# The first feed-forward block summed in six blocks of tiles instead of seven, and its list scheduler's weights set anew

## The chip, the cores and the metric

One core of a Trainium2 chip. Every time is in device microseconds (us) of that core; the time of a kernel is the median of its runs. The engines are called by their names: TensorE (PE, and PEld for its weight loads), VectorE (DVE), ScalarE (ACT), GpSimd (POOL), and SyncE (SP), which issues most DMAs.

## What is computed

Attention with a learned relative bias, then two feed-forward blocks without residuals. The change lies in the first of the two, `_moe_ref`, and in the way the second is cut:

```python
def _moe_ref(x, w_in, w_out, a, b):          # x 1152 x 512, w_in 512 x 2048, w_out 2048 x 512
    h = x @ w_in
    h2 = h * h
    h3 = h2 * h
    P = a[0] + a[1] * h + a[2] * h2 + a[3] * h3
    Q = 1.0 + np.abs(b[0]) * np.abs(h) + np.abs(b[1]) * h2
    g = P / (Q + 1e-06)
    return g @ w_out

def _moe2_ref(x, w_in, w_out):               # same sizes
    h = x @ w_in
    return np.maximum(0.01 * h, h) @ w_out
```

The weights come as 64-bit numbers.

## The kernel before

The attention takes the first 255 us or so. The feed-forward blocks work on the 2048 hidden features in 16 tiles f = 0 to 15 of 128 features, each over all 1152 tokens. Precision is kept by splitting every operand into a high and a low half, so a product is three matmuls (high x high, high x low, low x high).

**Per tile of the first block.** `gemm1(f, kk)` (L349 to L362) makes h of tile f in PSUM: 4 contractions x 3 products x 3 token chunks of 384 = 36 matmuls on L359. There are two such PSUM buffers, so `gemm1` of tile f waits until the last reader of tile f-2, `r_v`, is through. Then comes the rational function, in steps of one instruction each over 128 x 1152 (tile 15 in three chunks of 384):

- ScalarE: `r_abs` (L395), `r_s1` (L399), `r_qq` (L406), `r_ln` (L416), `r_exp` (L419), `r_q1` (L424), `split_hi` (L449).
- VectorE: `r_qa` (L403, needs `r_abs`), `r_h2` (L409, needs `r_s1`), `r_h3` (L412), `r_v` (L433, needs `r_h3` and `r_exp`), `r_fin` (L436, needs `r_v` and `r_e`).
- GpSimd: `r_e` (L430, needs `r_exp` and `r_q1`; for tiles 0 to 2 it is done on VectorE, L428) and `split_lo` (L454, needs `split_hi`).

`r_ln` and `r_exp` give 1/Q, `r_fin` the tile g, and `split_hi`/`split_lo` its two halves gh and gl, in a pool of buffers.

**Units.** The product g @ w_out is summed over blocks of tiles (`BLOCKS`, L138). For each block there are 12 units (n, c): 4 output groups x 3 token chunks. `g2_mm` (matmuls on L940) is a unit's 3 matmuls for each tile of the block, into one of two PSUM buffers; `g2_acc` takes the sum out: for the first block by a copy on ScalarE (L950), for every later one by an add on VectorE (L952). After the last block each result is split for the next product (L955 on ScalarE, L967 on VectorE).

**Weights.** Step t loads two weight tiles by DMA (`w_load`, SP), turns them from 64 to 32 bits by three VectorE steps (`w_dve`, L316, L318, L320), and splits them by `w_hi` (L330, ScalarE) and `w_lo` (L338, GpSimd).

**The order.** All engines take their instructions in the order in which the program issues them. For the first block, `plan_first` (L1002) writes every step down as a task with its engine, its cost (`COST`) and what it waits for, and `arrange` (L71) is a list scheduler: a task's rank is the longest chain behind it plus a number per kind of step from `SHIFT`; on the engine that can begin first it takes, of the tasks that can start within `SLACK` of that beginning, the one of the highest rank. The list that comes out is the order of issue. It begins after `gemm1` of tile 1; what is ahead is written out by hand. The second block (`g2_tok`, matmuls on L981, adds on L989) has a fixed plan by steps of a tile and uses the same `BLOCKS`.

Of the kernel before, what the change touches and what calls it, by code (L numbers as in the profile page):

```python
# [43 lines left out]
SHIFT = {'g2_acc': 85.7,
         'g2_mm': 40.9,
         'g2_out': 8.3,
         'gemm1': 162.0,
         'r_abs': 97.9,
         'r_e': -55.8,
         'r_exp': 33.0,  # L50
         'r_fin': -7.4,
         'r_h2': 273.8,
         'r_h3': -41.1,
         'r_ln': -206.8,
         'r_q1': 51.6,
         'r_qa': -51.7,
         'r_qq': 199.1,
         'r_s1': -20.3,
         'r_v': 10.2,
         'split_hi': 262.3,  # L60
         'split_lo': 61.1,
         'w_dve0': 177.5,
         'w_dve1': 15.3,
         'w_dve2': 11.6,
         'w_hi': 90.2,
         'w_lo': 57.9,
         'w_load': 106.7}
SLACK = 0.19


def arrange(tasks, ends, free):  # L71
# [63 lines left out]
]  # L135
MASK_BUFS = 20
LOAD_BUFS, EARLY = 3, 4
BLOCKS = [1, 2, 2, 2, 3, 3, 3]  # L138
NEX = 2
HI_MERGED = ()  # L140
LO_MERGED = ()
# [91 lines left out]
def attn_bias_moe_kernel(  # L233
# [131 lines left out]
    pools = {}  # L365
# [636 lines left out]
    def plan_first(rest, by_chunk):  # L1002
# [12 lines left out]
        units, held = [], {}  # L1015
# [5 lines left out]
        u_of = {bi: [u for u in units if u[0] == bi] for bi in range(len(blocks))}  # L1021
# [24 lines left out]
        for f in range(1, NF):  # L1046
            if f > 1:
                for kk in range(KD):
                    add(("gemm1", f, kk), [("gemm1", f, kk - 1) if kk else ("gemm1", f - 1, KD - 1)]
                        + [made.get(("i", f))] + [("r_v", *x) for x in parts(f - 2)])  # L1050
            part = 1 / len(parts(f))
            last = ("gemm1", f, KD - 1)
            for x in parts(f):
                c = x[1:]
                add(("r_abs", *x), [last, ("r_qa", f - 1)], part)
                add(("r_s1", *x), [last, ("split_lo", f - 3)], part)
                add(("r_qa", *x), [("r_abs", *x), ("r_fin", f - 3)], part)
# [12 lines left out]
                add(("split_lo", *x), [("split_hi", *x)], part)  # L1070
        before = []
# [13 lines left out]
    for m, plan, g2_lag, fn, args in (  # L1085
# [31 lines left out]
        for s in range(4 * (NF + 5)):  # L1117
# [5 lines left out]
            for step, name, *a in plan:  # L1123
                f, rem = divmod(s - step, 4)
# [80 lines left out]
```

## Time and profile before

| | us |
|---|---|
| median of 3 runs | 674.03 (673.1 to 675.94) |
| the profiled execution | 678.19, its span 676.4 |
| attention and the first tiles, to about | 256 |
| first feed-forward block, to | 472.1 |
| second feed-forward block, to the end | 676.4 |
| TensorE busy | 598.4 (88% of the span) |
| VectorE busy | 526.1 (78%) |
| ScalarE busy | 410.2 (61%) |
| GpSimd busy | 360.0 (53%) |

The table's busy times are averages over stages in which different engines set the pace, so they say little by themselves: the stage has to be read, and in it which wait ends last. A wait is idle time of an engine ahead of an instruction, put down to what released it.

### The profile page before, as it was taken

The page shows a single profiled execution, that of the slowest core. Times are in us where ns is not written, and L with a number is a line of the kernel's source. Part 1 is how long each engine was busy: PE and PEld are TensorE (multiplying, and loading weights), DVE is VectorE, ACT ScalarE, POOL GpSimd, SP SyncE. Part 2 cuts the span into 40 slices and gives each one's busy share as a digit, 9 for nine tenths or more (in the row PEclk, how much of TensorE's full clock was granted, in tenths as well). Part 3 has the DMA queues.
Part 4 walks back from the last instruction along what each step waited for, and adds up shares of the span by engine and source line. Part 5 has one row for each costly group of instructions (what it writes and reads, how often), then busy time and mean ns, then how long its engine had stood idle before and what let it go on. Part 6 is the DMA issues. An engine that isn't in the chain of part 4 may idle for free.

```text
span 676.4 us, 11799 instructions
## 1 busy us (share of the span) xinstructions
PE 598.4 (88%) x4595; PEld 528.8 (78%) x4595; DVE 526.1 (78%) x809; ACT 410.2 (61%) x625; POOL 360.0 (53%) x263
## 2 busy tenths in 40 slices
PE   5767778889888866779999998999999999999998
PEld 3333557778677856779998898999999999999876
DVE  7999889988979577888999999998256465645463
ACT  9999678888868357687687686754254223232210
POOL 5766687766756412467547565752154634453340
PEclk9998979998979788879999999999999999999999
DMA  5666799999969812113122211011132313230113
GB/s 191 185 165 189 214 158 205 210 189 194 160 127 175 192 62 89 67 63 125 62 71 71 108 63 63 31 64 63 48 112 91 125 63 111 76 125 31 60 50 125
DMA packets 102199, 77.35 MB, mean 114 GB/s; under 512 B 86400, under 2 KB 86784, under 8 KB 102144
## 3 DMA queue, kind: packets, MB, share of 16 engines
q1 hardware_dynamic: 100848, 68.97, 40.0%
q10 hardware_dynamic: 1296, 7.64, 3.5%
q8 instruction: 36, 0.59, 0.3%
q14 instruction: 19, 0.16, 0.1%
HBM read 42.39 MB, written 2.36 MB: 66 GB/s over the span
## 4 chain that ended last, share of the span: by engine, by line
PE 50%; DVE 25%; ACT 6%; issue 5%; DMA 3%; POOL 1%; SPq 0%; DVEq 0%; ACTq 0%; POOLq 0%
PE ph L359 20%; PE pz L981 13%; PE py L940 7%; PE ps L721 5%; DVE raw L320 2%; DVE ph L412 2%; DVE raw L318 2%; PE pv L813 2%; DVE raw L316 2%; DVE bias L952 2%; DMA biasr<-in_moe_w_in 2%; DVE s L433 2%; DVE s L436 2%; DVE pt L733 2%; DVE qq L403 1%
## 5 line engine op out<-in xcount | busy, mean ns | idle before, releaser
L359 PE MATMUL ph<-bias,bias 128*128 128x384 f32 x1152 | 218.5, 345 | 15.4 <-DVE s L433 12.8
L359 PEld LDWEIGHTS ph<-bias,bias 128*128 128x128 f32 x1152 | 209.5, 195 | 20.8 <-issue 12.8
L786 POOL TENSOR_TENSOR hl<-ex,hl 128x512 f16<-128x512 f32 (+2 forms) x94 | 91.5, 991 | 38.1 <-DVE hl L773 20.7
L454 POOL TENSOR_TENSOR gl<-s,gh 128x1152 fp32r<-128x1152 f32 (+1 forms) x33 | 85.5, 2595 | 35.6 <-ACT gh L449 35.1
L721 PE MATMUL ps<-kt,qz 128*128 128x288 f32 x432 | 80.9, 328 | 21.5 <-DVE mn L733 16.2
L721 PEld LDWEIGHTS ps<-kt,qz 128*128 128x128 f32 x432 | 64.6, 203 | 33.7 <-DVE mn L733 17.6
L338 POOL TENSOR_TENSOR bias<-raw,bias 128x512 fp32r<-128x512 f32 x37 | 49.1, 1329 | 74.9 <-ACT bias L330 74.9
L940 PE MATMUL py<-gh,wo 128*128 128x384 f32 x288 | 80.7, 340 | 4.0 <-DVE bias L952 3.4
L989 DVE TENSOR_TENSOR bias<-pz,bias 128x512 f32<-128x512 f32 x48 | 33.1, 689 | 59.8 <-PE pz L981 59.5
L981 PE MATMUL pz<-wo,gh 128*128 128x512 f32 (+1 forms) x240 | 74.4, 386 | 0.3 <-DVE bias L989 0.3
L338 POOL TENSOR_TENSOR wo<-raw,wo 128x512 fp32r<-128x512 f32 x23 | 30.3, 1318 | 78.1 <-ACT wo L330 78.0
L749 ACT ACTIVATE ex<-pt,mn 128x576 f32<-128x576 f32 x72 | 55.3, 768 | 19.0 <-DVE mn L733 15.3
L629 PEld LDWEIGHTS <-coef 128*32 128x32 f16 x1152 | 27.3, 99 | 41.9 <-issue 27.4
L647 POOL TENSOR_TENSOR t<-t,te 128x576 f32<-128x576 f32 x36 | 47.0, 1310 | 22.4 <-DVE bb L652 12.9
L940 PEld LDWEIGHTS py<-gh,wo 128*128 128x128 f32 x288 | 52.6, 188 | 8.1 <-DVE bias L952 6.2
L733 DVE CUSTOM_DVE_ANT_0 pt<-ps,bias 128x576 f32<-128x576 f32 x64 | 47.4, 744 | 6.7 <-PE ps L721 5.4
L330 ACT ACTIVATE wo<-raw 128x512 fp32r<-128x512 f32 x27 | 17.0, 629 | 58.1 <-DVE raw L320 58.1
L940 PE MATMUL py<-gl,wo 128*128 128x384 f32 x156 | 52.2, 335 | 0.0
L441 ACT ACTIVATE s<-ph 128x1152 f32<-128x1152 f32 x16 | 18.2, 1136 | 54.8 <-PE ph L359 43.5
L981 PEld LDWEIGHTS pz<-wo,gh 128*128 128x128 f32 x240 | 44.3, 188 | 8.2 <-DVE bias L989 0.7
L981 PE MATMUL pz<-wo,gl 128*128 128x512 f32 (+1 forms) x129 | 50.1, 389 | 0.0
L430 POOL TENSOR_TENSOR qq<-qq,r 128x1152 f32<-128x1152 f32 (+1 forms) x15 | 37.9, 2524 | 16.6 <-ACT r L419 12.0
(134 smaller groups left out, 1188.9 us busy)
## 6 DMA issues: line engine op xcount, KB each, us to landing
biasr<-in_moe_w_in SPq DMA_DIRECT2D x32, 512.0 KB, 4.4
biasr<-in_moe_w_out SPq DMA_DIRECT2D x32, 512.0 KB, 3.5
bias<-bb SPq DMA_DIRECT2D x32, 288.0 KB, 3.6
qkv<-in_qkv ACTq DMA_DIRECT2D x8, 896.0 KB, 5.2
out<-bias SPq DMA_DIRECT2D x8, 256.0 KB, 2.0
biasr<-bb SPq DMA_DIRECT2D x8, 144.0 KB, 4.0
et<-hl SPq DMA_TRANSPOSE x40, 4.8
sm<-in_small SPq DMA_DIRECT2D x1, 416.0 KB, 5.4
```

What stands on the lines that cost most here:

```text
L338: G.tensor_tensor(lo_, raw[:, x], hi_.bitcast(F32), ALU.subtract)
L359: PE.matmul(ps[:, c, 0:CH], w[:, sl], x[kk][:, c * CH:(c + 1) * CH], start=(kk == 0 and n == 0), stop=(kk == KD - 1 and n == 2),)
L430: G.tensor_tensor(part(qq[f], c), part(qq[f], c), part(r0[f], c), ALU.mult)
L454: eng.tensor_tensor(part(gl, c), part(s1[f], c), part(gh, c).bitcast(F32), ALU.subtract)
L647: G.tensor_tensor(t1, t0s.pop(n), te[:, S - first_row(n):2 * S - first_row(n)], ALU.mult)
L721: PE.matmul(ps[:, c, 0:288], lt[:, a], kts[i][:, b, 288 * c:288 * c + 288], start=(n == 0), stop=(n == 2),)
L733: V.tensor_tensor_reduce(out=c2(pt), in0=s_ps.pop((i, j))[:, :, 0:288], in1=c2(bsrc), op0=ALU.add, op1=ALU.min, scale=1.0, scalar=3.0e38, ...
L749: A.activation(et, pt, AF.Exp, bias=mn, scale=-1.0, accum_out=sums[i][:, col:col + 1],)
L786: engines[j in at].tensor_tensor(hl[:, xs, dst], e9[:, xs, src], hl[:, xs, src], ALU.subtract)
L940: PE.matmul(ps[:, 0:CH], w[:, sl], gts[f][x][:, cs], start=(f == f0 and m == 0), stop=(f == f0 + nf - 1 and m == 2),)
L981: PE.matmul(ps[:, half], gts[f][x][:, sl], w[:, half], start=(f == f0 and m == 0), stop=(f == f0 + nf - 1 and m == 2),)
L989: V.tensor_tensor(dst, ps[:, half], dst, ALU.add)
```

## The change

`BLOCKS` goes from [1, 2, 2, 2, 3, 3, 3] to [1, 3, 3, 3, 3, 3]: before, the tiles were summed as 0 | 1-2 | 3-4 | 5-6 | 7-9 | 10-12 | 13-15, now as 0 | 1-3 | 4-6 | 7-9 | 10-12 | 13-15. The buffers of split tiles, 2 x 3 = 6 before, become `G_BUFS` = 7, so that `split_hi` of tile f waits for the units of the block of tile f-7. All 24 numbers of `SHIFT` and `SLACK` are new (three are shown). One line more moves the line numbers behind L138 up by one.

```diff
-SHIFT = {'g2_acc': 85.7,
+SHIFT = {'g2_acc': 285.2,
...
-         'r_s1': -20.3,
+         'r_s1': 54.7,
...
-         'w_load': 106.7}
-SLACK = 0.19
+         'w_load': -193.4}
+SLACK = 0.34
...
-BLOCKS = [1, 2, 2, 2, 3, 3, 3]
+G_BUFS = 7
+BLOCKS = [1,3,3,3,3,3]
...
-    pools["g"] = ctx.enter_context(tc.tile_pool(name="gp", bufs=2 * max(BLOCKS)))
+    pools["g"] = ctx.enter_context(tc.tile_pool(name="gp", bufs=G_BUFS))
...
-                gone = [("g2_mm", *u) for u in u_of.get(held.get(f - 2 * max(BLOCKS)), ())]
+                gone = [("g2_mm", *u) for u in u_of.get(held.get(f - G_BUFS), ())]
```

What this does to the order of the engines, in three places. In the rows a name's number is that of the buffer; ph is h of a tile in PSUM, s1, qq and r0 are the rational function's tiles, bias2 is the running sum of the first block, raw and biasr are weights on their way.

ScalarE at tile 2 of the first block, from `r_abs` to `r_ln`, with the engines that each instruction waits for. Before:

```order
L395 ACTIVATE ah_4321<-ph_4265,babs_65 128x1152 [waits PE_49]
L330 ACTIVATE bias3_74<-raw_76 128x512 [waits Pool_49]
L950 ACTIVATE bias2_73<-py_4317 128x384 [waits PE_49]
L950 ACTIVATE bias2_73<-py_4323 128x384 [waits PE_49]
L399 ACTIVATE s1_4344<-ph_4265,nab_66 128x1152 [waits DVE_49]
L406 ACTIVATE qq_4330<-qq_4330 128x1152
L416 ACTIVATE r0_4358<-qq_4330,onep_67 128x1152 [waits Activation_49]
```

Now:

```order
L396 ACTIVATE ah_4327<-ph_4264,babs_65 128x1152 [waits PE_49]
L400 ACTIVATE s1_4329<-ph_4264,nab_66 128x1152
L951 ACTIVATE bias2_73<-py_4315 128x384 [waits PE_49]
L407 ACTIVATE qq_4331<-qq_4331 128x1152 [waits DVE_49]
L450 ACTIVATE gh_4358<-s1_4274 128x1152 [waits DVE_49]
L951 ACTIVATE bias2_73<-py_4321 128x384 [waits PE_49]
L417 ACTIVATE r0_4372<-qq_4331,onep_67 128x1152 [waits Activation_49]
```

`r_s1` (L399, now L400) stood behind two evictions and waited for VectorE's `r_qa`, which reads the same PSUM buffer and was issued ahead of it; now it follows `r_abs`, is issued ahead of `r_qa` and waits for nothing on VectorE. The same holds for tiles 1 to 5 and 14; for the others it was so before. `split_hi` of tile 1 (L450) now stands between `r_qq` and `r_ln`.

VectorE from `r_qa` of tile 4 to `r_qa` of tile 5. Before:

```order
L403 SCALAR_TENSOR_TENSOR qq_4479<-ah_4467,babs_65,ph_4404 128x1152
L409 TENSOR_TENSOR s1_4492<-ph_4404,s1_4492 128x1152
L412 SCALAR_TENSOR_TENSOR ph_4404<-s1_4492,nab_66,ph_4404 128x3x384
L316 TENSOR_SCALAR raw_76<-biasr_75 128x1024
L318 SCALAR_TENSOR_TENSOR raw_76<-biasr_75,raw_76 128x1024
L320 SCALAR_TENSOR_TENSOR raw_76<-biasr_75,raw_76 128x1024
L433 SCALAR_TENSOR_TENSOR s1_4492<-ph_4404,nab_66,r0_4507 128x1152
L403 SCALAR_TENSOR_TENSOR qq_4557<-ah_4536,babs_65,ph_4481 128x1152
```

Now:

```order
L404 SCALAR_TENSOR_TENSOR qq_4490<-ah_4475,babs_65,ph_4403 128x1152
L410 TENSOR_TENSOR s1_4488<-ph_4403,s1_4488 128x1152
L437 SCALAR_TENSOR_TENSOR s1_4413<-qq_4416,s1_4413 128x1152
L413 SCALAR_TENSOR_TENSOR ph_4403<-s1_4488,nab_66,ph_4403 128x3x384
L434 SCALAR_TENSOR_TENSOR s1_4488<-ph_4403,nab_66,r0_4516 128x1152
L317 TENSOR_SCALAR raw_76<-biasr_75 128x1024
L404 SCALAR_TENSOR_TENSOR qq_4569<-ah_4554,babs_65,ph_4478 128x1152
```

The three weight steps stood ahead of `r_v` (L433, now L434) and now begin behind it; `r_fin` of tile 3 (L437) stood behind `r_h2` of tile 5 before and now stands ahead of `r_h3` of tile 4.

VectorE between `r_h3` of tile 7 and `r_h2` of tile 8. Before:

```order
L412 SCALAR_TENSOR_TENSOR ph_4676<-s1_4789,nab_66,ph_4676 128x3x384
L316 TENSOR_SCALAR raw_76<-biasr_75 128x1024
L318 SCALAR_TENSOR_TENSOR raw_76<-biasr_75,raw_76 128x1024
L320 SCALAR_TENSOR_TENSOR raw_76<-biasr_75,raw_76 128x1024
L952 TENSOR_TENSOR bias2_73<-py_4851,bias2_73 128x384
L952 TENSOR_TENSOR bias2_73<-py_4861,bias2_73 128x384
L403 SCALAR_TENSOR_TENSOR qq_4882<-ah_4859,babs_65,ph_4802 128x1152
L952 TENSOR_TENSOR bias2_73<-py_4873,bias2_73 128x384
L952 TENSOR_TENSOR bias2_73<-py_4885,bias2_73 128x384
L433 SCALAR_TENSOR_TENSOR s1_4789<-ph_4676,nab_66,r0_4837 128x1152
L952 TENSOR_TENSOR bias2_73<-py_4896,bias2_73 128x384
L409 TENSOR_TENSOR s1_4905<-ph_4802,s1_4905 128x1152
```

Now, from the weight steps of the same tile on:

```order
L317 TENSOR_SCALAR raw_76<-biasr_75 128x1024
L319 SCALAR_TENSOR_TENSOR raw_76<-biasr_75,raw_76 128x1024
L321 SCALAR_TENSOR_TENSOR raw_76<-biasr_75,raw_76 128x1024
L437 SCALAR_TENSOR_TENSOR s1_4657<-qq_4683,s1_4657 128x1152
L413 SCALAR_TENSOR_TENSOR ph_4671<-s1_4777,nab_66,ph_4671 128x3x384
L953 TENSOR_TENSOR bias2_73<-py_4834,bias2_73 128x384
L434 SCALAR_TENSOR_TENSOR s1_4777<-ph_4671,nab_66,r0_4805 128x1152
L953 TENSOR_TENSOR bias2_73<-py_4850,bias2_73 128x384
L410 TENSOR_TENSOR s1_4865<-ph_4783,s1_4865 128x1152
```

Five adds (L952) stand in this piece before and two now, and the order is the same for every tile from here on: weight steps, `r_fin` of the tile before, `r_h3`, `r_v`, `r_qa` and `r_h2` of the next with adds between. Before, `r_fin` came up to two tiles late, in pairs.

On TensorE the units (matmuls on L940, now L941) that stand between the `gemm1` of the tiles are: before, one unit of two tiles between `gemm1` 5 and 6, then 6, 7, 6, 5, 5, 6 units of two tiles and 4, 3, 5 of three behind `gemm1` 6 to 14, and 24 units of three tiles behind `gemm1` 15; now none between `gemm1` 5 and 6, then 5, 4, 4, 3, 4, 3, 4, 4, 3 units of three tiles, and 26 behind `gemm1` 15. The 12 units of the first block stand where they stood. SP's order is the same.

## Rows read from the trace of the kernel before

**Rows 1.** The page's first line.

```profile
span 676.4 us, 11799 instructions
```

**Rows 2.** Busy time by stage: from:to, length, busy us of each engine (instructions), TensorE's clock, DMA.

```profile
core 0: us, PE busy (x) PEld busy (x) DVE busy (x) ACT busy (x) POOL busy (x), PEclk, DMA share, GB/s
...
295.30:300.00 4.70, 4.70 (x15) 4.70 (x16) 3.23 (x3) 3.42 (x3) 4.57 (x3) 0.50 0.02 5
...
320.20:426.70 106.50, 102.00 (x572) 98.28 (x571) 103.81 (x108) 75.56 (x73) 65.73 (x33) 1.00 0.20 70
...
433.00:472.10 39.10, 38.01 (x218) 37.29 (x217) 35.12 (x63) 20.25 (x38) 19.99 (x14) 1.00 0.17 58
472.10:676.40 204.30, 200.40 (x1018) 181.69 (x1016) 107.03 (x125) 57.87 (x71) 79.36 (x45) 1.00 0.24 84
```

**Rows 3.** Waits, 255 to 485: engine and line, for whom; us, times, longest.

```profile
PE ph L359 <- DVE s L433: 12.8, 4, 6.4
...
DVE s L409 <- ACT s L399: 7.5, 7, 1.4
```

**Rows 4.** VectorE's timeline: start, us, engine, line, out<-in, [idle before <- releaser].

```profile
271.33 1.40 DVE L433 SCALAR_TENSOR_TENSOR s<-ph,nab,r 128x1152 f32<-128x1152 f32 x1
272.66 1.40 DVE L403 SCALAR_TENSOR_TENSOR qq<-ah,babs,ph 128x1152 f32<-128x1152 f32 x1
275.44 1.36 DVE L409 TENSOR_TENSOR s<-ph,s 128x1152 f32<-128x1152 f32 x1 [1.38 <-ACT s L399]
...
282.42 1.41 DVE L433 SCALAR_TENSOR_TENSOR s<-ph,nab,r 128x1152 f32<-128x1152 f32 x1
...
293.72 1.42 DVE L433 SCALAR_TENSOR_TENSOR s<-ph,nab,r 128x1152 f32<-128x1152 f32 x1
...
303.74 1.41 DVE L433 SCALAR_TENSOR_TENSOR s<-ph,nab,r 128x1152 f32<-128x1152 f32 x1
...
318.31 1.41 DVE L433 SCALAR_TENSOR_TENSOR s<-ph,nab,r 128x1152 f32<-128x1152 f32 x1
```

**Rows 5.** ScalarE's timeline, `r_s1` of tiles 2 and 6.

```profile
274.09 1.31 ACT L399 ACTIVATE s<-ph,nab 128x1152 f32<-128x1152 f32 x1 [2.86 <-DVE qq L403]
...
316.83 1.31 ACT L399 ACTIVATE s<-ph,nab 128x1152 f32<-128x1152 f32 x1
```

**Rows 6.** TensorE's timeline: `gemm1` of tiles 5, 7, and the second block's first.

```profile
295.28 8.93 PE L359 MATMUL ph<-bias,bias 128*128 128x384 f32 x36 [3.78 <-DVE s L433]
...
320.17 6.40 PE L359 MATMUL ph<-bias,bias 128*128 128x384 f32 x36
...
485.31 12.75 PE L359 MATMUL ph<-bias,bias 128*128 128x384 f32 x72 [0.59 <-DVE s L444]
```

**Rows 7.** The chain that ended last: start, us, what; the last twelve units.

```profile
453.16 19.07 PE py L940 x108
```

**Rows 8.** VectorE's timeline, weight steps of two tiles.

```profile
364.98 2.10 DVE L316 TENSOR_SCALAR raw<-biasr 128x1024 int32<-128x1024 int32 x1
...
375.63 0.68 DVE L316 TENSOR_SCALAR raw<-biasr 128x1024 int32<-128x1024 int32 x1
376.35 1.23 DVE L318 SCALAR_TENSOR_TENSOR raw<-biasr,raw 128x1024 int32<-128x1024 int32 x1
377.61 1.22 DVE L320 SCALAR_TENSOR_TENSOR raw<-biasr,raw 128x1024 int32<-128x1024 int32 x1
```

**Rows 9.** Groups by line and form: xcount | busy us, mean ns | idle before.

```profile
L454 POOL TENSOR_TENSOR gl<-s,gh 128x1152 fp32r<-128x1152 f32 x30 | 82.1, 2740 | 34.3 <-ACT gh L449 33.8 <-DMA biasr<-in_moe_w_out 0.5
...
L952 DVE TENSOR_TENSOR bias<-py,bias 128x384 f32<-128x384 f32 x72 | 38.7, 551 | 4.6 <-PE py L940 4.5
L449 ACT ACTIVATE gh<-s 128x1152 fp32r<-128x1152 f32 x30 | 34.6, 1156 | 9.1 <-PE pz L981 4.6 <-DVE s L436 4.2
...
L316 DVE TENSOR_SCALAR raw<-biasr 128x1024 int32<-128x1024 int32 x24 | 22.5, 936 | 12.0 <-DMA biasr<-in_moe_w_in 12.0
```

**Rows 10.** POOL's timeline, `r_e` beside the first step of rows 8.

```profile
363.85 2.67 POOL L430 TENSOR_TENSOR qq<-qq,r 128x1152 f32<-128x1152 f32 x1
```

More of the change, by code (lines that the diff above doesn't have):

```diff
@@ L42 @@
 E_DVE_1 = ()
-SHIFT = {'g2_acc': 85.7,
[L45 to L57, printed above, removed]
-         'r_s1': -20.3,
[L59 to L66, printed above, removed]
-         'w_load': 106.7}
-SLACK = 0.19
+SHIFT = {'g2_acc': 285.2,
+         'g2_mm': 1.9,
+         'g2_out': 44.7,
+         'gemm1': 50.3,
+         'r_abs': 71.3,
+         'r_e': -48.0,
+         'r_exp': 178.1,
+         'r_fin': 2.1,
+         'r_h2': -90.6,
+         'r_h3': -51.4,
+         'r_ln': -196.5,
+         'r_q1': 110.6,
+         'r_qa': -99.6,
+         'r_qq': 49.4,
+         'r_s1': 54.7,
+         'r_v': 204.8,
+         'split_hi': 156.3,
+         'split_lo': 25.5,
+         'w_dve0': 46.3,
+         'w_dve1': 282.1,
+         'w_dve2': 149.1,
+         'w_hi': 297.1,
+         'w_lo': 17.0,
+         'w_load': -193.4}
+SLACK = 0.34
 def arrange(tasks, ends, free):
```

## The prediction

> **What bounds the kernel now.** Read first the span [rows 1], then the stages [rows 2]. The profiled execution took 678.19 us around a span of 676.4; the median of the three timed runs is 674.03, which is 4.16 less, so the sum below is made against 678.19 and taken off 674.03. What a measurement of this kernel can tell from no change is about 0.5%, 3.4 us. In the stretches of [rows 2] the reader sees three regimes. From 472.1 on (second feed-forward block) TensorE is busy 200.4 of 204.3 us: nothing done on the other engines can shorten it. From 320.2 to 426.7 (first block, tiles 7 to 14) VectorE is busy 103.8 of 106.5 us, and TensorE 102.0: both nearly full, VectorE a little fuller. From 433.0 to 472.1 TensorE is busy 38.0 of 39.1. Before that, between 266 and 305, TensorE waits: the waits of the stretch [rows 3] give 12.8 us in four pieces for `gemm1` (L359) waiting on `r_v` (L433), the step that frees its PSUM buffer. So the first tiles are a chain through VectorE, tiles 7 to 14 are limited by VectorE's sum of work, the rest by TensorE's.
>
> On VectorE the chain of the first tiles is in [rows 4]: `r_v` of tiles 1 to 5 starts at 271.33, 282.42, 293.72, 303.74 and 318.31. Inside each period `r_h2` (L409) stands behind `r_qa` (L403) and idles 1.38 us: qa starts at 272.66, h2 only at 275.44. [Rows 5] say why: ScalarE's `r_s1` (L399), which makes h2's input, starts at 274.09, when qa ends, after ScalarE stood still for 2.86 us with "DVE qq L403" named. For tile 6, where s1 is issued ahead of qa, it runs at 316.83 without such a wait, and h2 does not idle. Over the stretch h2's waits are 7.5 us in seven pieces [rows 3], of which 6.3 lie in tiles 1 to 5.
>
> **The change, part by part.** Prices: `gemm1` of one tile is 36 matmuls, at 72 in 12.75 us [rows 6] 6.37 us; a unit over three tiles is 9 matmuls, at 108 in 19.07 us [rows 7] 1.59 us, over two tiles 1.06.
>
> *(A) The first tiles, f 1 to 6.* In the new order s1 stands right behind `r_abs` and is issued ahead of qa, so h2's wait goes; `r_fin` moves to the place between qa and h2 (tile 2) or behind h2 (tile 4); in tile 2 `r_e` moves behind `r_v`; the three `w_dve` steps ahead of `r_v` of tile 4 (3.1 us: 0.68 + 1.23 + 1.22 [rows 8]) move behind it. Walked with the rows' durations on VectorE, and with ScalarE's queue beside it: v1 starts 0.8 us earlier (h2's wait of 1.38 less about 0.6 for a weight half that now precedes `r_abs`). From v1 to v2 11.1 us become 8.6: 1.38 of wait and 1.33 of `r_e` go, 0.2 is waited for `r_exp`. From v2 to v3 11.3 become 11.2 (`r_e` comes in, the wait goes out). From v3 to v4 10.0 become 7.7: 1.4 of wait and 3.1 of weights go, 1.3 of `r_fin` comes in, and 0.9 is waited for `r_exp`, since ScalarE now has `split_hi` and `r_q1` of earlier tiles to do on the way to it. From v4 to v5 14.6 become 14.9: the weight steps stand there now, and the first adds wait for the first units behind `gemm1` 6. Together -0.8 -2.5 -0.1 -2.3 +0.3 = **-5.4 us** at v5, and `gemm1` of tile 7, at 320.17 before [rows 6], follows v5. Block 1 now needs tile 3 and starts behind `gemm1` of tile 6 instead of one unit ahead of it; by the start of `gemm1` 7 the order has 5 units of three tiles done (15 tile shares) where before it had 7 of two (14), so no work is pushed back there. Ends: 0, if another wait takes each place; -8.0, if `gemm1` 5 also keeps the full clock. That one took 8.93 us, 2.6 above its price, after 3.78 us of idle TensorE, with the granted clock at 0.50 (1.2 GHz) from 295.3 to 300.0 [rows 2, 6]; in the walk the idle time ahead of it is 2.8, little shorter, and I keep the slow one.
>
> *(B) Tiles 7 to 14.* Between the starts of `gemm1` 7 and 15 the order had 41 units, now 29: twelve adds (L952) fewer, 0.551 us each alone [rows 9]; the next instruction starts up to 0.1 before an instruction's recorded end, so 0.51 is taken. VectorE is what fills the 106.5 us, so they count in full: 12 x 0.51 = **-6.1 us**, leaving 100.4. Ends: 0 on the weak side; on the strong side TensorE's own work, 8 x 6.37 + 29 x 1.59 = 97.1 us, so no more than -9.4. I take -6.1 because the stretch's own busy share speaks for VectorE, and 100.4 lies above TensorE's 97.1.
>
> *(C) The tail.* Behind `gemm1` 15 there are 26 units of three tiles instead of 24: TensorE was busy 38.0 of 39.1 us there [rows 2], so two units cost 2 x 1.59 = **+3.2 us**. Ends: +3.2 and, if evictions stall two more units, +4.5.
>
> *(D) The second block* is also cut into six. Its matmuls are the same number, TensorE idles there once for 0.59 us [rows 6], and both ends are set at 0 and +1: nine fewer adds on an engine with time to spare. The seventh buffer of split tiles costs nothing: the tile whose buffer it reuses belongs to a block whose units stand ahead in TensorE's order. The DMAs and SP's order are the same as before.
>
> Sum: -5.4 - 6.1 + 3.2 + 0 = **-8.3 us**: 669.9 for an execution like the profiled one, **665.7** as a median.
>
> A point weighed against a rule. `w_dve0` (L316) at 364.98 took 2.10 us, the same step at 375.63 0.68: in the first case `r_e` on POOL ran from 363.85 to 366.52, and VectorE's step ended 0.56 after it, at 367.08 [rows 8, 10]. The Trainium skill, "SBUF — State Buffer", section "Who interferes with whom", says that the port pair shared by VectorE and GpSimd is a lock for a whole instruction, the later one waiting in full; by that rule, which this row bears out, B depends on where POOL's work falls. If the eight first weight steps of the stretch met none of it, at a mean of 936 against 680 ns [rows 8, 9], 2.0 us more would go (663.7); if each met it as at 364.98, 8 x 1.42 = 11.4 would come back (677.1). In the walk `r_e` ends at or before the weight steps, so I leave the mean as it is.
>
> **The rivals.** *TensorE becomes the bound* (in stretch B everything VectorE does is hidden): -5.4 - 9.4 + 3.2 = -11.6, 662.4. For it: 102.0 us busy there already. Against: the adds and `r_v` wait for each other in order, which costs something. *The first tiles gain nothing* (ScalarE's longer run ahead of `r_exp` eats A): -6.1 + 3.2 = -2.9, 671.1. For it: the walk already waits 0.2 and 0.9 on `r_exp`. *ScalarE sets the pace of tiles 6 to 14*: in the new order two weight halves, `split_hi` and `r_q1` stand ahead of `r_abs`. From the end of the weight steps `r_abs` ends after fin, then hi, q1 and abs, 1.36 + 1.16 + 1.31 + 1.31 = 5.1 us (fin at the row of h2, q1 and abs at that of s1, an upper bound); VectorE has fin, h3, add, v, add before qa, 1.36 + 1.40 + 0.51 + 1.40 + 0.51 = 5.2 us [rows 4, 5, 9]. A margin of 0.1; 1 us more per tile, nine times, would take the whole gain back: about 674, no change. *Slower*: `r_fin` now stands directly behind the weight steps and ahead of h3 and v, one tile after its `r_v` instead of up to two, and it needs `r_e` from POOL, which waits for `split_lo`, which waits for `split_hi`, which waits for the `r_fin` before. That loop is 2.67 + 1.36 + 1.16 + 2.74 = 7.9 us [rows 4, 9, 10], in a period of 100.4 / 8 = 12.5. If `r_e` is late by more than (8.3 + 3.4) / 9 = 1.3 us at each of nine tiles, every `r_v` and `gemm1` behind it is late by that and the kernel is slower; at 1.6 us it ends at 674.03 - 8.3 + 14.4 = 680.1. Against it: 4.6 us of room for POOL's two weight halves and the hand-overs.
>
> **How the numbers follow.** Forecast 0.50; TensorE the bound 0.22; first tiles gain nothing 0.12; ScalarE's pace, no change, 0.09; slower 0.07. The third lies on the edge of 670.7, half of it counts as faster: faster 0.50 + 0.22 + 0.06 = 0.78, same 0.06 + 0.09 = 0.15, slower 0.07. The range takes in the first three cases: down to 660.0 (TensorE the bound, and most of the 2.6 us of A's strong end), up to 672.0 (the third case and a run's scatter); left out are the last two, and a little of the first end, together under 0.2.
>
> **What would show it.** In the changed profile: h2's waits on s1 (7.5 us) down to about 1; `r_v` of tile 5 near 313 and `gemm1` 7 near 315; from there to `gemm1` 15 some 100 us, with 60 adds in the program where 72 were; the first block ends (start of the second's `gemm1`, 472.1 now) near 464; the second block still 204 us. The prediction is wrong in A if h2's idle time turns up as waits of `r_v` on `r_exp`, in B if VectorE waits for `r_e` or `r_abs`, in C if more than 1.5 us of idle time stands between the last units, and in D if TensorE idles anywhere behind the first block.

## The result, and the profile after

| us | before | after | forecast of the difference | measured |
|---|---|---|---|---|
| median | 674.99 (4 runs, 673.1 to 679.19) | 666.84 (4 runs, 664.18 to 669.17) | -8.3 | -8.15 |
| profiled execution, its span | 678.19, 676.4 | 666.41, 664.6 | | |
| start of `gemm1` of tile 2 | 258.51 | 253.35 | 0 | -5.16 |
| A: from there to `gemm1` of tile 7 | 61.66 | 60.61 | -5.4 | -1.05 |
| B: to `gemm1` of tile 15 | 106.48 | 96.65 | -6.1 | -9.83 |
| C: to the second block's first `gemm1` | 45.42 | 48.84 | +3.2 | +3.42 |
| D: to the end | 204.33 | 205.15 | 0 | +0.82 |

After over before is 0.989, with a 95% interval of 0.9848 to 0.9932. The total came as forecast, but not by the forecast's sum: A gave a fifth of what it should, B a good half more. The four stretches add up to -6.64 us, which lies within that interval (-4.6 to -10.3 us); the 1.5 us between that and the medians' difference are within the scatter. The start of `gemm1` of tile 2 is no effect of the change: in the profiles of this study it lies anywhere from 253.6 to 258.5 with the first tiles of before, and from 252.7 to 258.5 with those of the changed kernel or an edit of them. So stretches are compared here, not ends. It also brought two signs of the forecast near by chance: `r_v` of tile 5 at 312.06 (forecast near 313) and `gemm1` of tile 7 at 313.96 (near 315) came mostly from the early start, not from A. B repeats to 0.5 us: in the changed kernel and the six runs that leave its steps in B alone it was 96.34 to 96.82. A repeats less well: with the first tiles of before it was 61.66 to 61.84 in four executions, with those of after 60.61 and, in experiment 7, 59.69.

Every experiment was timed beside the kernel before, and its median is to be held against that one: 672.87 us for experiments 1 to 4, 674.11 for 5 to 8, 672.97 for 9 to 11, 674.01 for 12.

The stretches A, B, C and D of the changed kernel, and then B and C together (columns: from:to, length, busy us of each engine with its instructions, TensorE's clock, DMA share, GB/s):

```profile
253.35:313.96 60.61, 48.83 (x250) 47.96 (x250) 52.94 (x44) 48.03 (x52) 30.61 (x16) 0.88 0.23 78
313.96:410.61 96.65, 96.11 (x551) 95.00 (x550) 92.19 (x93) 72.66 (x72) 63.38 (x32) 1.00 0.23 82
410.61:459.45 48.84, 47.65 (x272) 46.62 (x271) 45.76 (x75) 27.24 (x44) 26.54 (x16) 1.00 0.17 55
459.45:664.60 205.15, 201.15 (x1018) 182.02 (x1017) 103.98 (x118) 57.84 (x73) 80.54 (x46) 1.00 0.24 86
...
313.96:459.45 145.49, 143.75 (x821) 141.62 (x820) 137.95 (x167) 99.90 (x115) 89.92 (x47) 1.00 0.21 73
```

B and C together in the kernel before:

```profile
320.17:472.07 151.90, 146.31 (x823) 141.87 (x823) 145.19 (x177) 101.16 (x115) 89.50 (x47) 1.00 0.20 67
```

Read the second row against the row of tiles 7 to 14 in [rows 2]: there TensorE was busy 102.0 of 106.5 us and VectorE 103.8; now TensorE is busy 96.1 of 96.65, so its own work is a bound, and VectorE has 4.5 us of idle time (experiment 3 shows how little of that is free). TensorE also has 21 matmuls fewer there (572 before), and 19 more in C (253 before): units moved back. B and C together hold the same work on TensorE (823 and 821 matmuls), and this is the clean comparison: 151.90 us became 145.49. TensorE's idle time there went from 5.6 to 1.7 us, its busy time from 146.3 to 143.75 (in B the matmuls of gh by wo, the largest group of the units, took 342 ns on the mean and now take 337). VectorE's busy time went down by 7.2.

**Where VectorE's time in B went.** Groups of the kernel before in B (mean ns of one behind the bar):

```profile
L952 DVE TENSOR_TENSOR bias<-py,bias 128x384 f32<-128x384 f32 x41 | 21.8, 550 | 1.0 <-PE py L940 0.9
L320 DVE SCALAR_TENSOR_TENSOR raw<-biasr,raw 128x1024 int32<-128x1024 int32 x7 | 10.9, 1559 | 0.2
L316 DVE TENSOR_SCALAR raw<-biasr 128x1024 int32<-128x1024 int32 x7 | 8.7, 1245 | 0.6 <-DMA biasr<-in_moe_w_in 0.6
```

The worst of these steps, and the `r_e` of GpSimd beside it:

```profile
406.65 3.58 DVE L320 SCALAR_TENSOR_TENSOR raw<-biasr,raw 128x1024 int32<-128x1024 int32 x1
...
405.98 3.17 POOL L430 TENSOR_TENSOR qq<-qq,r 128x1152 f32<-128x1152 f32 x1 [1.18 <-PE ph L359]
```

The groups in the changed kernel:

```profile
L953 DVE TENSOR_TENSOR bias<-py,bias 128x384 f32<-128x384 f32 x29 | 15.9, 551 | 2.0 <-PE py L941 1.9
L321 DVE SCALAR_TENSOR_TENSOR raw<-biasr,raw 128x1024 int32<-128x1024 int32 x8 | 9.8, 1225 | 0.3
L317 DVE TENSOR_SCALAR raw<-biasr 128x1024 int32<-128x1024 int32 x8 | 6.8, 850 | 0.0
```

Twelve adds went, as counted: 5.9 us. But the weight steps are shorter too, from 1559 to 1225 ns and from 1245 to 850: before, five of them met an `r_e` of GpSimd and lost 6.3 us (over the 0.68 and 1.23 that they take alone), now the loss is 1.4. This was in the sum of the prediction at nothing.

**Why A gave so little.** VectorE's timeline in A after (start, us, what, [idle before <- releaser]):

```profile
257.46 1.42 DVE L404 SCALAR_TENSOR_TENSOR qq<-ah,babs,ph 128x1152 f32<-128x1152 f32 x1 [3.79 <-ACT s L400]
...
266.41 1.41 DVE L434 SCALAR_TENSOR_TENSOR s<-ph,nab,r 128x1152 f32<-128x1152 f32 x1
...
271.59 0.41 DVE L317 TENSOR_SCALAR raw<-biasr 128x512 int32<-128x512 int32 x1
272.04 3.05 DVE L319 SCALAR_TENSOR_TENSOR raw<-biasr,raw 128x512 int32<-128x512 int32 x1
275.12 0.69 DVE L321 SCALAR_TENSOR_TENSOR raw<-biasr,raw 128x512 int32<-128x512 int32 x1
...
277.25 1.42 DVE L434 SCALAR_TENSOR_TENSOR s<-ph,nab,r 128x1152 f32<-128x1152 f32 x1
...
288.41 1.42 DVE L434 SCALAR_TENSOR_TENSOR s<-ph,nab,r 128x1152 f32<-128x1152 f32 x1
...
290.82 1.42 DVE L404 SCALAR_TENSOR_TENSOR qq<-ah,babs,ph 128x1152 f32<-128x1152 f32 x1 [0.99 <-ACT s L400]
...
293.42 2.35 DVE L437 SCALAR_TENSOR_TENSOR s<-qq,s 128x1152 f32<-128x1152 f32 x1
...
297.21 1.42 DVE L434 SCALAR_TENSOR_TENSOR s<-ph,nab,r 128x1152 f32<-128x1152 f32 x1
...
312.06 1.40 DVE L434 SCALAR_TENSOR_TENSOR s<-ph,nab,r 128x1152 f32<-128x1152 f32 x1
```

GpSimd beside it, `split_lo` of tile 1:

```profile
271.68 2.86 POOL L455 TENSOR_TENSOR gl<-s,gh 128x1152 fp32r<-128x1152 f32 x1 [4.07 <-ACT gh L450]
```

Waits of A, the view of [rows 3]:

```profile
PE ph L360 <- DVE s L434: 11.8, 3, 6.6
...
DVE qq L404 <- ACT s L400: 5.8, 3, 3.8
```

`r_v` of tiles 1, 2 and 3 starts 13.06, 23.90 and 35.06 us behind `gemm1` of tile 2; before it was 12.82, 23.91 and 35.21 [rows 4, against 258.51]. Nothing was gained up to there. Two things stand in the rows: h2 no longer waits for `r_s1`, but `r_qa` does (L404, 3.79 and 0.99); and the weight step at 272.04, which takes 0.69 us alone, took 3.05, because GpSimd's `split_lo` got in between it and the step ahead.

The start of `gemm1` of tile 5, which follows `r_v` of tile 3, repeats to 0.02 us in kernels with equal first tiles: 36.76 to 36.77 behind `gemm1` of tile 2 with those of before (four profiles), 36.63 to 36.65 with those of after (three). From that start on TensorE works without a gap to `gemm1` of tile 7 in the changed kernel, and the time there differs with the clock: 23.98 us at a mean granted clock of 0.88 here, 23.04 at 0.93 in another execution with the same first tiles (experiment 7). In both it is at the lower level (0.50, 1.2 GHz) near the start of this piece, here behind 3.61 us of idle TensorE. So below, the first tiles are read at `gemm1` of tile 5.

### The profile page after: what moved, and what is told of

Read it like the earlier page. It is cut to its first block, busy times and chain, and to the rows that moved or that the text cites. A ratio compares the mean times of both kernels' runs of the same rounds, so it can differ in the third digit from the quotient of the medians.

```text
span 664.6 us, 11791 instructions
## 1 busy us (share of the span) xinstructions
PE 593.9 (89%) x4595; PEld 527.5 (79%) x4595; DVE 514.6 (77%) x788; ACT 408.7 (61%) x625; POOL 360.5 (54%) x263
## 3 DMA queue, kind: packets, MB, share of 16 engines
HBM read 42.39 MB, written 2.36 MB: 67 GB/s over the span
## 4 chain that ended last, share of the span: by engine, by line
PE 54%; DVE 18%; DMA 6%; ACT 5%; issue 5%; POOL 2%; SPq 0%; DVEq 0%; POOLq 0%; ACTq 0%
PE ph L360 21%; PE pz L982 13%; PE py L941 11%; PE ps L722 5%; DMA biasr<-in_moe_w_in 3%; DVE raw L319 3%; DVE raw L317 2%; PE pv L814 2%; DVE raw L321 2%; DMA et<-hl 2%; ACT ex L750 1%; DVE pt L734 1%; DMA qkv<-in_qkv 1%; PE pr L841 1%; DVE ph L413 1%
## 5 line engine op out<-in xcount | busy, mean ns | idle before, releaser
L360 PE MATMUL ph<-bias,bias 128*128 128x384 f32 x1152 | 215.9, 341 | 14.6 <-DVE s L434 11.8
L360 PEld LDWEIGHTS ph<-bias,bias 128*128 128x128 f32 x1152 | 206.5, 192 | 20.3 <-ACT bias L951 6.9
L455 POOL TENSOR_TENSOR gl<-s,gh 128x1152 fp32r<-128x1152 f32 (+1 forms) x33 | 84.1, 2548 | 11.5 <-ACT gh L450 11.0
L339 POOL TENSOR_TENSOR bias<-raw,bias 128x512 fp32r<-128x512 f32 x37 | 51.1, 1382 | 58.7 <-ACT bias L331 48.5
L941 PE MATMUL py<-gh,wo 128*128 128x384 f32 x288 | 78.7, 337 | 1.7 <-DVE bias L953 1.6
L990 DVE TENSOR_TENSOR bias<-pz,bias 128x512 f32<-128x512 f32 x40 | 27.6, 690 | 52.9 <-PE pz L982 52.9
L941 PEld LDWEIGHTS py<-gh,wo 128*128 128x128 f32 x288 | 52.5, 188 | 3.7 <-DVE bias L953 3.6
L317 DVE TENSOR_SCALAR raw<-biasr 128x1024 int32<-128x1024 int32 (+1 forms) x40 | 33.6, 841 | 24.0 <-DMA biasr<-in_moe_w_in 22.6
L941 PE MATMUL py<-gl,wo 128*128 128x384 f32 x156 | 52.2, 334 | 0.0
```

The source lines that it names most:

```text
L317: V.tensor_scalar(bits, hi32, 3, 0x3FFFFFF8, ALU.logical_shift_left, ALU.bitwise_and)
L339: G.tensor_tensor(lo_, raw[:, x], hi_.bitcast(F32), ALU.subtract)
L360: PE.matmul(ps[:, c, 0:CH], w[:, sl], x[kk][:, c * CH:(c + 1) * CH], start=(kk == 0 and n == 0), stop=(kk == KD - 1 and n == 2),)
L455: eng.tensor_tensor(part(gl, c), part(s1[f], c), part(gh, c).bitcast(F32), ALU.subtract)
L941: PE.matmul(ps[:, 0:CH], w[:, sl], gts[f][x][:, cs], start=(f == f0 and m == 0), stop=(f == f0 + nf - 1 and m == 2),)
```

## Experiments

**1. The place of `r_s1`.** The changed kernel, and:

```diff
-            for k in plan_first(args, by_chunk):
+            seq = plan_first(args, by_chunk)
+            for f in range(1, 6):
+                seq.remove(("r_s1", f))
+                seq.insert(seq.index(("r_qa", f)) + 1, ("r_s1", f))
+            for k in seq:
```

> The changed kernel, with r_s1 of tiles 1 to 5 issued right behind r_qa instead of ahead of it, as it stood before the change; nothing else in the order is different. Theory 1 (r_s1 and r_qa read the same PSUM buffer and are taken in the order of issue; whichever comes second waits out the first, so the place of r_s1 only decides where the wait shows): the waits of r_qa on r_s1 (8.0 us in six pieces in the changed kernel) go, r_h2's waits on r_s1 come back (about 6 us), and from gemm1 of tile 2 to gemm1 of tile 7 it takes 60.6 us give or take 1. Rival (the prediction's term A: the wait of h2 was worth 1.4 us a tile, and its removal was eaten by something else): the stretch grows by about 5 us, to 65 or 66. The rest of the kernel is as in the changed one under both, so the total is 666 to 668 against 671 to 672.

A was 60.62 us, the changed kernel's 60.61; B, C and D were 96.82, 48.84 and 204.9, the median 668.85 (665.58 to 672.71). The waits changed places as theory 1 says; the waits of A, and two lines of VectorE's timeline:

```profile
DVE s L410 <- ACT s L400: 5.7, 4, 1.4
...
DVE qq L404 <- ACT ah L396: 2.6, 1, 2.6
...
271.90 0.69 DVE L319 SCALAR_TENSOR_TENSOR raw<-biasr,raw 128x512 int32<-128x512 int32 x1
...
281.16 1.36 DVE L410 TENSOR_TENSOR s<-ph,s 128x1152 f32<-128x1152 f32 x1 [1.39 <-ACT s L400]
```

At `gemm1` of tile 5 it was 0.56 us behind (37.19). But the equal A is partly luck, since the edit moved something else too: `split_lo` of tile 1 now comes at 272.70, and the weight step at 271.90 takes its 0.69 us. So 2.36 us of collision went, and the place of `r_s1` took about as much back. `r_v` of tiles 1, 2 and 3 starts 13.35, 22.67 and 35.62 us behind `gemm1` of tile 2. At tile 1 the place only chose who waits (0.29 us); at tile 3, where h2 idles 1.39 us again, the step from `r_v` of tile 2 took 12.95 us for 11.16. The prediction's price for that edit, 1.4 us a tile, falls at tile 1 and stands at tile 3.

**2. That wait taken away.** The changed kernel, and:

```diff
-        A.activation(part3(s1[f], c), hp(f, c), AF.Identity, bias=nab[:, 2:3], scale=nab[:, 3:4])
+        src = part3(ah[f], c) if 1 <= f < 6 else hp(f, c)
+        A.activation(part3(s1[f], c), src, AF.Identity, bias=nab[:, 2:3], scale=nab[:, 3:4])
```

> The changed kernel, with r_s1 of tiles 1 to 5 reading the SBUF tile that r_abs wrote instead of the PSUM buffer of h, so that r_qa no longer shares an operand with it; order and sizes are the same. It leaves out the sign of h in that one term. Theory 1 (the wait for a shared PSUM reader is a real cost of about 1.2 us a tile in the first tiles): r_qa's waits on r_s1 go for these five tiles, and from gemm1 of tile 2 to gemm1 of tile 7 it takes 3 to 5 us less than the changed kernel's 60.6. Rival (collisions with GpSimd, or ScalarE's own chain to r_exp, set the pace there): less than 1 us is gained, because r_v then waits for r_exp. The total is 662 to 664 by the first, 666 to 667 by the second.

A was 58.66, 1.95 less: between the two. VectorE's timeline shows that `r_qa` now runs beside `r_s1` and starts when `r_abs` ends:

```profile
257.20 1.41 DVE L405 SCALAR_TENSOR_TENSOR qq<-ah,babs,ph 128x1152 f32<-128x1152 f32 x1 [2.60 <-ACT ah L396]
...
288.21 1.42 DVE L435 SCALAR_TENSOR_TENSOR s<-ph,nab,r 128x1152 f32<-128x1152 f32 x1
```

The expectation counted five waits; ahead of `gemm1` of tile 5 the changed kernel has only the one at tile 1 (3.79, now 2.60), since at tiles 2 and 3 other work of VectorE, `r_e` above all, fills that time. `gemm1` of tile 5 came 1.13 us sooner (35.50), the 1.2 of that one wait; the rest of the 1.95 lies behind it, where the clock differs. The median was 665.6.

**3 and 4. The adds, put in and taken out.** In the changed kernel:

```diff
+            if bi in (1, 2) and (n + c) % 2 == 0:
+                V.tensor_tensor(dst, ps[:, 0:CH], dst, ALU.add)
```

> The changed kernel, with twelve of the VectorE adds of blocks 1 and 2 (every second unit) done twice in a row; it adds those partial sums twice. That is as many adds in the first block's tiles 7 to 14 as the kernel before had. Theory 1 (TensorE is what bounds the changed kernel from gemm1 of tile 7 to gemm1 of tile 15, 96.7 us there): VectorE has 4 us or so to spare and the stretch grows by 1 to 3 us. Rival (VectorE bounds it, as the prediction had it): it grows by 12 x 0.51 = 6.1 us, to 102.8. Of the twelve some one or two may fall ahead of gemm1 of tile 7. The total is 668 to 670 against 673.

In the kernel before:

```diff
-        else:
+        elif not (bi in (2, 3) and (n + c) % 2 == 0):
```

> The kernel before, with the VectorE add left out for twelve units of blocks 2 and 3 (tiles 3 to 6; every second unit); its order and its blocks are otherwise those of before, and those partial sums are missing. Theory 1 (the number of adds was what the kernel before paid for in tiles 7 to 14): from gemm1 of tile 7 to gemm1 of tile 15 the 106.5 us become 100 to 102 (not less, as some of the twelve lie ahead of tile 7, which then starts up to 1.5 us sooner). Rival (the gain of the change in that stretch came from the new order of the steps, not from the number of adds): the stretch stays at 105 to 107. The total is 667 to 669 against 673 to 675.

In both the rival's number came. Put in, the adds cost about their full time: B was 102.52, 5.87 more, with 11 VectorE instructions more in it, A 62.29, and the median 674.37. Experiment 3, B:

```profile
316.65:419.17 102.52, 97.49 (x550) 94.85 (x550) 98.86 (x104) 72.60 (x72) 61.96 (x32) 1.00 0.21 78
```

VectorE's busy time grew by 6.67 us, 11 adds and 1.5 us more lost on weight steps beside GpSimd; its idle time fell only from 4.5 to 3.7, and TensorE's rose from 0.5 to 5.0. So little of VectorE's idle time in B was free: in the changed kernel both engines are nearly full there. The second add also holds its PSUM buffer longer, and TensorE waits for it (3.2 us of its weight loads, 2.1 of its matmuls); how the cost divides between that and VectorE's sum this run can't tell.

Taken out, they brought nothing: B 106.40, C 46.01, median 674.56 (672.87 before). Windows of the kernel of experiment 4, B and C together, then one stretch of tile 13 and a piece of it, and the matmul behind the gap:

```profile
318.05:470.46 152.41, 147.54 (x824) 143.59 (x823) 140.79 (x165) 101.00 (x115) 89.97 (x47) 0.99 0.19 66
...
396.00:410.00 14.00, 12.07 (x65) 11.75 (x64) 13.93 (x11) 8.21 (x8) 10.89 (x5) 0.92 0.11 37
408.00:410.00 2.00, 2.00 (x8) 2.00 (x8) 2.00 (x3) 0.00 (x0) 1.91 (x2) 0.50 0.59 229
...
407.15 0.45 PE L940 MATMUL py<-gh,bias 128*128 128x384 f32 x1 [1.93 <-DVE bias L952]
```

VectorE had 4.4 us less to do in B and C, but the weight steps now met more of GpSimd's work (7.5 us lost in B, 6.3 before), and up to `gemm1` of tile 12 only 1.95 us had been gained (64.80 against 66.75). That was lost again behind an idle time of TensorE of 1.93 us at 405.2, after which its clock fell to the lower level: 0.50 (1.2 GHz) from 408 to 410, and a mean of 0.95 in the 14 us after. The kernel before has 1.00 behind a like idle time of 1.75:

```profile
410.75 0.45 PE L940 MATMUL py<-gh,bias 128*128 128x384 f32 x1 [1.75 <-DVE bias L952]
```

Whether the clock falls in every execution of experiment 4 is not known, since one was profiled; the median of its ten runs shows no gain either.

**5 and 6. Each half of the change alone.** The changed kernel with the 24 weights of before, and with the blocks and six buffers of before:

```diff
-SHIFT = {'g2_acc': 285.2,
+SHIFT = {'g2_acc': 85.7,
...
-SLACK = 0.34
+SLACK = 0.19
```

> The changed kernel's blocks and seven buffers with the scheduler's weights of before; the list scheduler makes quite another order of it. From gemm1 of tile 7 to the second block's first gemm1 it took 151.9 us before and takes 145.5 in the changed kernel. Theory 1 (twelve adds fewer on VectorE are what pays there): 146 to 148 us. Rival (what pays is that the new weights put the weight steps of VectorE where GpSimd does not work: their time over the undisturbed 0.68 or 1.23 us is 6.3 us in tiles 7 to 14 before and 1.4 in the changed kernel): 150 us or more, with over 4 us of such extra time.

```diff
-G_BUFS = 7
-BLOCKS = [1,3,3,3,3,3]
+G_BUFS = 6
+BLOCKS = [1, 2, 2, 2, 3, 3, 3]
```

> The blocks and six buffers of before with the scheduler's new weights. From gemm1 of tile 7 to the second block's first gemm1, 151.9 us before and 145.5 in the changed kernel: theory 1 (the number of adds) 150 to 152 us; rival (the new order without collisions between VectorE's weight steps and GpSimd) 146 to 148 us, with under 3 us of extra time on the weight steps of tiles 7 to 14. The first tiles, which the number of adds touches little, should take 60 to 62 us from gemm1 of tile 2 to gemm1 of tile 7 under both.

Neither theory holds: both are slower than the kernel before, 688.28 us (1.0196, interval 1.0142 to 1.0251) and 689.99 (1.0233, 1.0165 to 1.03). Experiment 5 took more than the 150 us of its rival, but not for the rival's reason: the weight steps lost 2.5 us in tiles 7 to 14, not over 4. In experiment 6 they lost 5.9, and A was 59.50, just under the 60 to 62 expected. From `gemm1` of tile 7 to the second block, experiment 5:

```profile
319.57:483.02 163.45, 154.71 (x855) 151.50 (x856) 142.87 (x169) 99.59 (x113) 93.25 (x47) 0.97 0.17 59
```

There are 34 matmuls more in it than in the changed kernel: the order pushes units behind `gemm1` of tile 7 (215 matmuls in A, where the changed kernel has 250). TensorE idles 8.7 us (1.7 in the changed kernel), and its clock falls twice. Experiment 6, the same stretch and its first part:

```profile
312.28:480.26 167.98, 154.32 (x829) 147.69 (x829) 153.54 (x180) 101.84 (x116) 90.49 (x47) 0.96 0.19 63
...
312.28:337.00 24.72, 20.57 (x97) 19.02 (x97) 22.09 (x22) 10.63 (x10) 10.43 (x5) 0.83 0.12 43
```

Here units of two tiles stand in a row ahead of `gemm1` of tile 8, four of them wait for adds (0.35 to 2.00 us), and the clock falls to 0.83. So these weights fit their own block list, and the gain can't be divided between the two halves.

**7. Six buffers.** The changed kernel with `G_BUFS = 6`.

> The changed kernel with six buffers of split tiles instead of seven. Theory (the seventh buffer costs and brings nothing, since the units that free the sixth stand ahead in TensorE's order): 145 to 147 us from gemm1 of tile 7 to the second block's first gemm1, as with seven (145.5), total 664 to 669. Rival (split_hi then waits for the units of the block before, and POOL and r_e behind it): a wait of split_hi on TensorE of 1 us or more per block shows, and the stretch grows by 3 us or more.

B and C took 145.63 us, the median was 666.81, and `split_hi` waits for nothing on TensorE: the seventh buffer costs and brings nothing that these runs could tell, as forecast.

**8. `r_e` off VectorE.** The changed kernel with `E_DVE = (0,)` for `(0, 1, 2)`.

> The changed kernel with r_e of tiles 1 and 2 on GpSimd, as for the later tiles, and their r_q1 on ScalarE, instead of both on VectorE; the order of issue is otherwise the same. VectorE has some 3.4 us less to do between gemm1 of tile 2 and gemm1 of tile 7 (60.6 us in the changed kernel). Theory 1 (VectorE's own work is what these tiles cost): 57.5 to 58.5 us there, total 663 to 665. Rival (r_e on GpSimd comes later or meets VectorE's long instructions, and ScalarE's r_q1 delays the next r_abs): 60 to 61.5 us, total 666 to 668.

A was 59.56, but `gemm1` of tile 5 came only 0.14 us sooner (36.49); the median was 667.99. VectorE's timeline at tiles 2 and 3:

```profile
272.26 1.42 DVE L404 SCALAR_TENSOR_TENSOR qq<-ah,babs,ph 128x1152 f32<-128x1152 f32 x1 [0.98 <-ACT s L400]
...
284.91 1.41 DVE L404 SCALAR_TENSOR_TENSOR qq<-ah,babs,ph 128x1152 f32<-128x1152 f32 x1 [1.35 <-ACT s L400]
```

Of the 3.4 us taken off VectorE 2.33 came back as the wait that `r_e` had covered, and the collision at L319 stayed (3.06). A lies between the two, the total in the rival's range, and at `gemm1` of tile 5 next to nothing was gained: the rival comes nearer.

**9 and 10. GpSimd's part taken out of the kernel before**, without and with the edit of experiment 4:

```diff
             for k in plan_first(args, by_chunk):
+                if k[0] == "r_e" and k[1] in (6, 8, 10, 11, 12):
+                    continue
```

> The kernel before, with r_e of tiles 6, 8, 10, 11 and 12 left out (so their g is finished without that last factor of Q); these are the five GpSimd instructions beside which VectorE's weight steps took longer than 0.68 or 1.23 us in tiles 7 to 14, 6.3 us in all; the order of everything else is that of before. Theory 1 (VectorE's time lost beside GpSimd is what the kernel before pays for in that stretch): from gemm1 of tile 7 to gemm1 of tile 15, 106.5 us before, 100.5 to 102.5, the lower end being TensorE's own 572 matmuls. Rival (as with the twelve adds left out, which left 106.4: relieving VectorE brings nothing while the order of the steps stays): 104.5 to 107 us.

> The kernel before, with both left out: the twelve adds of blocks 2 and 3, and r_e of tiles 6, 8, 10, 11 and 12. Theory 1 (adds and time lost beside GpSimd together are what VectorE had too much, and behind them stands TensorE): from gemm1 of tile 7 to the second block's first gemm1, 151.9 us before and 145.5 in the changed kernel, it takes 145 to 147 us, with TensorE idle under 1.5 us. Rival (the order of the steps itself, not VectorE's sum of work, makes TensorE wait): 149 us or more.

Experiment 9, B and C:

```profile
316.78:465.42 148.64, 145.30 (x824) 142.07 (x824) 139.02 (x177) 101.03 (x115) 75.61 (x42) 1.00 0.19 68
```

Experiment 10:

```profile
315.40:463.03 147.63, 145.16 (x823) 142.24 (x823) 133.77 (x165) 101.04 (x115) 75.54 (x42) 1.00 0.19 68
```

B was 103.26 and 101.77 us (106.48 before), the medians 671.88 and 669.29. With the five `r_e` out no weight step loses time in B. Alone they bring 3.2 us there, half of the 6.3 that they had cost VectorE; the twelve adds, which alone brought nothing, bring 1.5 more on top. (Leaving `r_e` out also takes work off GpSimd; but in B of the kernel before neither VectorE nor TensorE waited for GpSimd by semaphore, so it is unlikely that the time comes from there.) Both times lie between theory and rival: with VectorE relieved by 11.4 us in B and C, 2.1 of the 6.4 us to the changed kernel (145.49) are still missing, and TensorE still idles 2.5 us. What is left over is the order of the steps and units, by elimination; no run shows which step's place is to blame.

**11 and 12. The first tiles mended.** Experiment 11 is the changed kernel with `E_DVE = (0, 2)` and, in the list:

```diff
+            for k, at in (("split_lo", 1), ("w_lo", 2, 0)), (("r_fin", 3), ("r_h3", 4)):
+                seq.remove(k)
+                seq.insert(seq.index(at) + 1, k)
```

> The changed kernel with three edits in its first tiles that leave all work in: r_e of tile 1 on GpSimd; split_lo of tile 1 behind GpSimd's weight half of step 2, so that VectorE's weight step (3.05 us beside it, 0.69 alone) no longer meets it; and r_fin of tile 3 behind r_h3 of tile 4, where VectorE would wait for r_exp. Theory (VectorE's collisions and waits are what these tiles cost): from gemm1 of tile 2 to gemm1 of tile 7, 60.6 us in the changed kernel, 56 to 58 us; total 662 to 664. Rival (ScalarE's chain to r_exp is right behind and takes over): 59 to 60 us, total 665 to 667.

A was 60.10, the median 665.39. These are the rival's numbers but not its reason: no `r_v` waits for `r_exp` here. VectorE's timeline:

```profile
274.97 1.42 DVE L434 SCALAR_TENSOR_TENSOR s<-ph,nab,r 128x1152 f32<-128x1152 f32 x1
276.31 3.83 DVE L429 SCALAR_TENSOR_TENSOR qq<-qq,onep,r 128x1152 f32<-128x1152 f32 x1
```

GpSimd's `split_lo` of tile 1 in its new place:

```profile
276.26 2.66 POOL L455 TENSOR_TENSOR gl<-s,gh 128x1152 fp32r<-128x1152 f32 x1
```

`r_v` of tile 2 came at 21.26, 2.64 us sooner, so the collision at 272.04 was what had eaten A's largest term. (`r_e` of tile 1 went too; in experiment 8, where it goes without the move, `r_v` of tile 2 came at 23.64, so 2.38 of the 2.64 are the collision's.) But the next VectorE instruction, `r_e` of tile 2 (1.41 alone), met the moved `split_lo` and gave 2.4 us back. Experiment 12 takes that `r_e` to GpSimd as well (`E_DVE = (0,)`) and leaves `r_fin` where it was:

> The changed kernel with r_e of tiles 1 and 2 on GpSimd and split_lo of tile 1 behind GpSimd's weight half of step 2; all work stays in. In the run before this one r_v of tile 2 came 2.6 us sooner than in the changed kernel, and the next VectorE instruction, r_e of tile 2, lost 2.4 us of it beside the moved split_lo; here that r_e is no longer VectorE's. Theory (gemm1 of tile 5 follows r_v of tile 3, and from its start TensorE works without a gap for 23 to 24 us to gemm1 of tile 7, so only what brings r_v of tile 3 forward counts): r_v of tile 3 33 to 34 us behind the start of gemm1 of tile 2 (35.1 in the changed kernel), gemm1 of tile 7 at 58 to 59 us (60.6), total 664 to 665.5. Rival (the time lost only moves on to the next weight step, beside r_e of tile 2 on GpSimd): r_v of tile 3 at 35 us, gemm1 of tile 7 at 59.5 to 60.6, total 665.5 to 667.

The theory holds: `r_v` of tile 3 at 33.64, `gemm1` of tile 5 at 35.21, of tile 7 at 58.01. VectorE's timeline:

```profile
275.70 1.42 DVE L434 SCALAR_TENSOR_TENSOR s<-ph,nab,r 128x1152 f32<-128x1152 f32 x1
279.14 1.42 DVE L404 SCALAR_TENSOR_TENSOR qq<-ah,babs,ph 128x1152 f32<-128x1152 f32 x1 [2.02 <-ACT s L400]
...
281.74 1.11 DVE L317 TENSOR_SCALAR raw<-biasr 128x1024 int32<-128x1024 int32 x1
...
288.07 1.42 DVE L434 SCALAR_TENSOR_TENSOR s<-ph,nab,r 128x1152 f32<-128x1152 f32 x1
```

Against experiment 8, from which it differs by the place of `split_lo` alone, `r_v` of tile 2 came 2.37 us sooner and `gemm1` of tile 5 1.28: of a collision of 2.4 us a good half reached TensorE. The median was 664.40 (0.9879 of before, interval 0.9839 to 0.9919). The stretch tells it from the changed kernel by 1.4 us at `gemm1` of tile 5; the totals, whose intervals overlap, do not.

## Why the prediction was right, and where it was wrong

- **The total** was right by luck: two errors of near size met. A was forecast 4.35 us too good, B 3.73 us too bad.
- **A failed, most of all in the step from `r_v` of tile 1 to that of tile 2.** The five terms -0.8, -2.5, -0.1, -2.3 and +0.3 came out as +0.24, -0.25, -0.14, -1.22 and +0.28. In that step "11.1 us become 8.6", and 10.84 were measured. The place of `r_s1` and of `r_e` brought what was said, but `split_hi` of tile 1, moved forward with `r_fin`, released GpSimd's `split_lo` at 271.68, just at a weight step of VectorE, which cost 2.36 us; experiments 11 and 12 showed that term by moving it. The prediction had put such collisions at nothing in A. The step ahead of it failed too ("v1 starts 0.8 us earlier", measured 0.24 later): the removed wait of h2 came back as a wait of `r_qa`. Both read h of the tile in PSUM and the program lets the second reader wait for the first, so at tile 1 moving `r_s1` only chose who waits (experiments 1 and 2); at tile 3, where `r_e` fills the gap, it gained what was said. The Trainium skill, "PSUM — Partial Sum Buffer", section "PSUM bank collisions raise a hardware error", says that two engines may not access one bank at a time in the same partitions, reads included, and that software has to keep them apart; the rows agree in so far as `r_qa` starts when `r_s1` ends. From `r_v` of tile 3 to that of tile 4 the 0.9 us of wait for `r_exp` did not come; 0.99 of `r_qa` waiting for `r_s1` and 1.0 of `r_fin` beside GpSimd (2.35 for 1.35 at 293.42) did. But the terms behind tile 3 had no effect of their own: from `gemm1` of tile 5 on TensorE runs without a gap. Of A's 1.05 us 0.14 were gained up to there and 0.91 behind it.
- **B was mis-sized.** Twelve adds fewer were counted right, 5.9 us of VectorE's time, but by experiments 4, 9 and 10 that alone was not what held B before: there the loss beside GpSimd came first. The term that failed is the one that the prediction left out of its sum. It weighed that loss by a rule on the shared port pair, with 2.0 us to gain at most; VectorE lost 4.9 less (6.3 before, 1.4 after). It took the mean of the first weight steps over the whole program, 936 ns, where those of the stretch have 1245, and it looked at the first steps only, while the largest loss was on a third one (3.58 us at 406.65 for 1.23). The rows agree with the rule itself: the step at 406.65 came second and ended 1.08 us behind the `r_e`, about its own length. What the change did in B was to lower adds and losses at once, in an order that lets TensorE run through; that the order has a part of its own (2.1 us in B and C) was only found as a remainder. Then the rival "TensorE becomes the bound" gave the time, 96.65 against its forecast 97.1, though VectorE has little to spare either (experiment 3).
- **C was right** (+3.42 for +3.2), for the reason given: 272 matmuls where 253 were. **D** lay within its ends.
- **The loop through `r_fin` and GpSimd, and ScalarE's pace,** did not show as costs: VectorE's waits in B are 1.9 us for units and 1.8 for `r_s1`, none for `r_e` or `r_abs`.

## What to carry to other kernels

A step moved on one engine moves all that it releases on the others: ask where each released GpSimd instruction will fall on VectorE's line, for one collision can eat the whole gain. Where two engines are nearly full, the time comes from both lists of work and from what they lose beside each other; taking one part away can show nothing (the adds alone), and the gain ends at the other engine's sum. A total that comes as forecast proves no term of the sum: compare stretch by stretch. The weights of a list scheduler belonged to one problem here: with another block list they made the kernel 2% slower than the one before.

## What was unexpected of the hardware

GpSimd gets in between two VectorE instructions that stand back to back: `split_lo` at 271.68 came while a weight step of 0.41 us ran, took 0.19 longer than its 2.67, and the next step, ready at 272.04, ended 0.55 us behind it at 275.09. Moved to 276.26, it cost the `r_e` at 276.31 another 2.42. And TensorE's clock fell to 0.50 behind an idle time of 1.93 us in one kernel and stayed at 1.00 behind 1.75 in another.
